# Loads issued only while about 1.4 MB of loads are under way, in a fused attention and two-layer kernel

## Chip, cores, metric

The kernel runs on one core of a Trainium2 chip. The metric is device time of one execution in microseconds (us); smaller is better. The profile is one profiled execution of the same program. Engines: PE does the matmuls, PEld is its weight load, DVE and ACT do vector work, POOL is GpSimd, and SP only issues DMAs and waits. A name with a q (SPq) is the sequencer of that engine.

## What is computed

Attention over chunks of 32 queries, each with 56 keys around it (16 to the left, 8 to the right) and 8 memory keys, for 4 batches, 8 heads, 768 positions, head width 64. Its output, 3072 tokens of 512, goes through two dense layers with a leaky activation. The reference, cut to what matters:

```python
for c in range(nc):                                   # 24 chunks of 32 queries
    q_c = q[:, :, c_start:c_end]
    k_full = np.concatenate([mem_k, k[:, :, l_start:r_end]], axis=2)
    v_full = np.concatenate([mem_v, v[:, :, l_start:r_end]], axis=2)
    scores = scale * np.matmul(q_c, k_full.transpose(0, 1, 3, 2))
    a = np.exp(scores - np.max(scores, axis=-1, keepdims=True))
    a = a / (np.sum(a, axis=-1, keepdims=True) + 1e-09)
    out[:, :, c_start:c_end] = np.matmul(a, v_full)
x = out.transpose(0, 2, 1, 3).reshape(B * S, H * D)   # 3072 x 512
h = x @ w_in                                          # 512 -> 2048
g = np.maximum(h, 0.0) + alpha * np.minimum(h, 0.0)
return g @ w_out                                      # 2048 -> 512
```

## The kernel before

**Attention.** The work is cut into 32 units: eight half sequences of 384 tokens times four pairs of heads. The first eight units (u < NWIN) take a path of their own, `windows`: score products on PE (`score_products`, L312, tile s_ps, with filler matmuls `stir`, L298, ahead of them), maximum, difference and sum on DVE, exponent on ACT (L517), scaling on POOL, a turn on PE (L546), two copies on ACT (L551), value products on PE (L559, tile a_ps), and a split of the result into a high part on ACT (xh, L474) and a low part on DVE (xl, L477). The other 24 units come later, spread over the dense layers (L337, L438).

**Dense layers.** The 2048 hidden columns are cut into 16 chunks f of 128. For a block of tokens and a chunk, PE makes h (12 matmuls, L723, 384 or 512 tokens wide) and adds to the output (L753). Every operand is two parts, high and low, so that three products stand for one. The first two blocks run jointly over the first nine chunks: (block 0, f), then (block 1, f - 1); then block 0 alone; then the others. Weights arrive as raw 64-bit words, 512 KB for a chunk of w_in and 512 KB for one of w_out, and are decoded once on ACT and DVE (`decode_part`, L622 to L649, first read of a load: L622) into parts that stay in the SBUF.

**Order.** Steps are entered into a `Plan` with a cost, what they read and write, and a due time. `Plan.send` lists them into one static order per engine before the program is built. At run time each engine goes through its list in that order and waits on semaphores; what stands behind a waiting instruction waits too.

**Loads.** All of them are issued by SP, in order:
- `load_first(u)` (L485): two loads for each of the first eight units from the tensor `first`: queries and keys (656 KB, here K0 to K7), and values (256 KB, here V0 to V7). They share four buffers `early`, so the loads of unit u + 4 wait until PE has read those of unit u. The DMA instruction is on L490.
- `load_w(f)` (L594): the two weight loads of chunk f (here I for w_in and O for w_out, each 512 KB), DMA on L599.
- alpha (8 KB), and for the later units `load_unit` (qvw and kw, L277, L280) and `load_v` (L290); the outputs at L818 and L822.

A DMA's completion is counted on one of eight semaphores in turn, and a DMA waits for the one that had its semaphore eight DMAs earlier.

SP's order at the beginning: K0, K1, K2, K3, K4, K5, V0, I0, K6, V2, V1, O0, K7, V4, V3, alpha, I1, V6, V5, I2, V7, O1, O2, I3, O3, I4, and on with weights.

Of the kernel before, what the change touches and what calls it, by code (L numbers as in the profile page):

```python
# [100 lines left out]


STIR = (8, 2, 1)

DUE_WEIGHTS, LAST_OUT = 4, 8

# [75 lines left out]
def body(ctx: ExitStack, tc: tile.TileContext, qvw, kw, first, w_in, w_out, alpha, out):  # L182
    nc = tc.nc
# [5 lines left out]
    at = ctx.enter_context(tc.tile_pool(name="at", bufs=1))  # L189
# [59 lines left out]
    def rest(place):  # L249
        wide = NNARROW * NF  # L250
        return (len(ORDER) - max(place, wide)) * WIDE_PAIR + max(wide - place, 0) * PAIR
# [5 lines left out]
    def due(u, later=0):  # L257

        return rest(begins(u) + later + (5.5 if u >= FIRST_FRONT else 0))
# [7 lines left out]

    def den_keys(u):
        return [("den", u % 3, n) for n in range(NJ * 2)]

    def load_unit(u):
        blk, pr = divmod(u, NPAIR)
        state[u] = {}
        i = sets(u)

        def load_q():
            nc.sync.dma_start(out=qs[i], in_=qvw[blk, pr, :, :BT])  # L277

        def load_k():
            nc.sync.dma_start(out=kbs[i], in_=kw[blk, pr])  # L280

        step(SP, 0.65, load_q, writes=[("q", i)], rest=due(u))
        step(SP, 0.81, load_k, writes=[("k", i)], rest=due(u))
# [11 lines left out]
    def stir(t, num):  # L295

        for _ in range(num):
            nc.tensor.matmul(out=t, lhsT=busy[:, :P], rhs=busy, start=True, stop=True)  # L298

    def score_products(u):  # L300
        blk, pr = divmod(u, NPAIR)
        st = state[u]
        s_ps = ps_s.tile([P, 512], F32, name="s_ps", tag=f"s{u % 2}")
        stir(s_ps, STIR[0] if u == 0 else STIR[1])
        st["s"] = s_ps[:, :2 * NJ * KW].rearrange("p (n k) -> p n k", k=KW)
# [45 lines left out]
    def scores(us):  # L351
        d = {}
        mk = ("mx", us[0] // len(us) % 2)

        def top(h2):
            if h2 == 0:
                d["mx"] = sm.tile([P, len(us), NJ, 2], F32, name="mx", tag=f"mx{len(us)}{mk[1]}")
            s = state[us[0]]["all"][h2]
            hide(us[0], s)
            nc.vector.tensor_reduce(out=d["mx"][:, :, :, h2], in_=s, axis=AX.X, op=ALU.max)  # L360

        def negate():
            nc.vector.tensor_scalar(out=d["mx"], in0=d["mx"], scalar1=-SCALE, scalar2=None, op0=ALU.mult)  # L363

        def exps(u, i):
            st = state[u]
            if i == 0:
                st["e"] = at.tile([P, NJ * 2, KW], F32, name="e", tag=f"e{u % 2}")
                st["den"] = sm.tile([P, NJ * 2, 1], F32, name="den", tag=f"den{u % 3}")
            n, h2 = divmod(i, 2)  # L370
            nc.scalar.activation(out=st["e"][:, i], in_=st["s"][h2][:, n], func=AF.Exp, scale=SCALE,  # L371
                                 bias=d["mx"][:, u - us[0], n, h2:h2 + 1], accum_out=st["den"][:, i])

        for h2 in range(2):
            step(DVE, 0.26 + 0.21 * len(us), partial(top, h2), writes=[("s", h2), mk], rest=due(us[0]))
        step(DVE, 0.17, negate, writes=[mk], rest=due(us[0]))
        for u in us:
            for i in range(NJ * 2):
                step(ACT, 0.54, partial(exps, u, i), reads=[("s", i % 2), mk],
                     writes=[("e", u % 2, i), ("den", u % 3, i)] if i else e_keys(u) + den_keys(u), rest=due(u))  # L380

    def weights(u):
        st = state[u]

        def guard():
            nc.vector.tensor_scalar(out=st["den"], in0=st["den"], scalar1=1e-9, scalar2=None, op0=ALU.add)

        def inverse():
            nc.vector.reciprocal(out=st["den"], in_=st["den"])  # L389

        def scale():
            nc.gpsimd.tensor_tensor(out=st["e"], in0=st["e"], in1=st["den"].broadcast_to([P, NJ * 2, KW]),  # L392
                                    op=ALU.mult)

        def spread():
            nc.scalar.copy(out=zeroed["e2"][:, :, NM:NM + CH], in_=st["e"][:, :, :CH])

        step(DVE, 0.16, guard, writes=den_keys(u), rest=due(u, DUE_WEIGHTS))
        step(DVE, 0.19, inverse, writes=den_keys(u), rest=due(u, DUE_WEIGHTS))
        step(POOL, 0.86, scale, reads=den_keys(u), writes=e_keys(u), rest=due(u, DUE_WEIGHTS))  # L400
        step(ACT, 0.37, spread, reads=e_keys(u), writes=["e2"], rest=due(u, DUE_WEIGHTS))
# [83 lines left out]
    def load_first(u):  # L485
        blk, pr = divmod(u, NPAIR)
        t = early[u % NSET]

        def load(lo, hi):
            nc.sync.dma_start(out=t[:, lo:hi], in_=first[blk, pr, :, lo:hi])  # L490

        state[u] = {}
        step(SP, 1.6, partial(load, 0, NQ + NT * NKT), writes=[("qk", u % NSET)], rest=due(u))
        step(SP, 0.78, partial(load, NQ + NT * NKT, NQ + NT * NKT + NV), writes=[("fv", u % NSET)], rest=due(u))

    def windows(u):
# [44 lines left out]
        def turn():  # L541
            st["t"] = [ps_o.tile([P, DM], F32, name="o_ps", tag=f"o{i}") for i in range(2)]
            stir(st["t"][0], STIR[2])
            for t in range(2):
# [43 lines left out]
    srcs = (w_in.bitcast(I32), w_out.bitcast(I32))  # L588

    raw = {}  # L590
# [3 lines left out]
    def load_w(f):  # L594
        def load(i):
            k, j = ((f, i), 0) if f < NAPART else ((f, 0), i)
            if k not in raw:
                raw[k] = wps[k].tile([P, 2 if f >= NAPART else 1, DM, 2], I32, name="w_t", tag="w")
            nc.sync.dma_start(out=raw[k][:, j].rearrange("p m b -> p (m b)"), in_=srcs[i][f])  # L599

        i = f - NF + NSET
        after = [("qk", i), ("fv", i)] if i >= 0 else []
        for i in range(2):
            step(SP, 1.31, partial(load, i), writes=[("r", f, i)] + after, rest=rest(place_of(f)))

    def place_of(f):
        return PLACE[0, f]
# [350 lines left out]
```

## Time and profile before

| what | us |
|---|---|
| three runs | 599.35, 599.86, 600.5 (median 599.86) |
| span of the profiled execution, from its first to its last instruction | 597.5 |
| median less span | 2.4 |
| PE busy in the span | 591.1 |

The profile has no other time of the profiled execution than its span; the 2.4 us are the median's distance from it, which holds what lies before the first and behind the last instruction. The granted clock of PE is 1.000. In the span 41.95 MB are read from HBM.

Start of the issue of the first loads, in us from the start of the span, by SP's rows:

| load | K0 | K1 | K2 | K3 | K4 | K5 | V0 | I0 | K6 | V2 | V1 | O0 | K7 | V4 | V3 |
|---|---|---|---|---|---|---|---|---|---|---|---|---|---|---|---|
| issued | 0.74 | 1.17 | 1.64 | 2.11 | 5.83 | 7.34 | 7.72 | 8.20 | 8.99 | 9.36 | 9.84 | 10.31 | 11.34 | 16.35 | 16.73 |

A row of the chain of work reads: start, length, what; it is followed back from the end to whatever released each step. A row of waits reads: who waited for whom, us in total, times, longest. A row of DMA issues gives the number of loads, the size of one and the median time from the start of its issue to its landing, when its semaphore is up.

### The profile page before, as it was taken

To read this page: it belongs to the slowest core of one execution; us is meant where nothing else is said; L and a number is where in the kernel's file an instruction comes from. 1 tells how busy PE (TensorE), PEld (TensorE's weight loads), DVE (VectorE), ACT (ScalarE), POOL (GpSimd) and SP (SyncE) were. 2 spreads that over 40 slices of the span, in tenths; PEclk is the share of its full clock that TensorE was granted. 3 is DMA by queue.
4 is the path that set the end of the run, shared out by engine and by line. 5 is a ranking of instruction groups with operands and counts; after the bars stand their busy time and mean duration, and the time that the engine had idled before them with its cause. 6 is when DMAs were issued, how large, how long until landed. Compare 5 with 4: busy or idle time off the path is not lost.

```text
span 597.5 us, 10975 instructions
## 1 busy us (share of the span) xinstructions
PE 591.1 (99%) x4430; PEld 505.7 (85%) x4430; DVE 386.7 (65%) x904; ACT 210.6 (35%) x580; POOL 36.5 (6%) x61
## 2 busy tenths in 40 slices
PE   8999999999999999999999999999999999999997
PEld 4789999888998989989898888888888888888885
DVE  5888898887959768685885852861862771530530
ACT  3788888644222504323233302302400411210201
POOL 3510000010001101010010100100100100000000
PEclk9999999999999999999999999999999999999999
DMA  8999500222040302403304003003101000000001
GB/s 337 359 399 407 226 0 1 66 65 89 2 152 2 101 23 79 153 1 100 94 8 150 4 1 100 2 0 109 62 2 36 1 0 36 36 1 0 1 1 71
DMA packets 21076, 48.96 MB, mean 82 GB/s; under 512 B 2464, under 2 KB 5792, under 8 KB 21024
## 3 DMA queue, kind: packets, MB, share of 16 engines
q1 hardware_dynamic: 20880, 48.12, 22.8%
q8 instruction: 35, 0.57, 0.4%
q14 instruction: 17, 0.14, 0.1%
q10 hardware_dynamic: 144, 0.13, 0.1%
HBM read 41.95 MB, written 6.29 MB: 81 GB/s over the span
## 4 chain that ended last, share of the span: by engine, by line
PE 96%; DMA 3%; SPq 0%; ACT 0%; issue 0%; ACTq 0%
PE h_ps L723 45%; PE o_ps L753 44%; PE a_ps L438 3%; DMA early<-first 3%; PE s_ps L337 2%; PE a_ps L559 1%; PE o_ps L546 1%; PE s_ps L312 0%; SPq L490 0%; PE o_ps L298 0%; ACT o_t L810 0%; PE s_ps L298 0%; ACTq L810 0%
## 5 line engine op out<-in xcount | busy, mean ns | idle before, releaser
L723 PE MATMUL h_ps<-xh,w 128*128 128x384 f32 (+1 forms) x896 | 248.8, 358 | 0.0
L723 PEld LDWEIGHTS h_ps<-xh,w 128*128 128x128 f32 x896 | 164.9, 188 | 16.0
L753 PE MATMUL o_ps<-w,gh 128*128 128x512 f32 x528 | 162.7, 389 | 0.0
L723 PE MATMUL h_ps<-xl,w 128*128 128x384 f32 (+1 forms) x448 | 162.6, 363 | 0.0
L732 ACT ACTIVATE g<-h_ps 128x384 f32<-128x384 f32 (+1 forms) x112 | 60.4, 540 | 194.7 <-PE h_ps L723 129.1
L735 DVE SCALAR_TENSOR_TENSOR g<-g,rise,h_ps 128x384 f32<-128x384 f32 (+1 forms) x112 | 74.7, 668 | 74.8 <-ACT g L732 74.1
L753 PEld LDWEIGHTS o_ps<-w,gh 128*128 128x128 f32 x528 | 99.1, 188 | 20.4
L413 DVE STREAM_TRANSPOSE pt<-e 32x64 f32<-32x64 f32 (+1 forms) x336 | 99.4, 301 | 7.4 <-POOL e L392 2.0
L753 PE MATMUL o_ps<-w,gl 128*128 128x512 f32 x264 | 102.8, 389 | 0.0
L723 PEld LDWEIGHTS h_ps<-xl,w 128*128 128x128 f32 x448 | 84.1, 188 | 10.2
L753 PE MATMUL o_ps<-w,xh 128*128 128x512 f32 x240 | 74.8, 393 | 0.0
L753 PEld LDWEIGHTS o_ps<-w,gl 128*128 128x128 f32 x264 | 49.6, 188 | 10.2
L477 DVE TENSOR_TENSOR xl<-a_ps,xh 128x384 fp32r<-128x384 f32 x32 | 17.6, 554 | 61.0 <-ACT xh L474 60.4
L753 PEld LDWEIGHTS o_ps<-w,xh 128*128 128x128 f32 x240 | 45.0, 188 | 8.9
L741 DVE CAST gh<-g 128x512 fp32r<-128x512 f32 (+1 forms) x72 | 28.8, 401 | 30.6 <-PE o_ps L753 28.2
L474 ACT CAST xh<-a_ps 128x384 fp32r<-128x384 f32 x32 | 15.0, 483 | 95.0 <-PE a_ps L438 93.7
L392 POOL TENSOR_TENSOR e<-e,den 128x384 f32<-128x384 f32 x24 | 22.8, 949 | 419.6 <-DVE den L389 270.0
L745 DVE TENSOR_TENSOR gl<-g,gh 128x512 fp32r<-128x512 f32 (+1 forms) x72 | 46.6, 648 | 1.7
L371 ACT ACTIVATE e<-s_ps,mx 128x64 f32<-128x64 f32 x144 | 43.4, 318 | 11.1 <-DVE mx L363 11.1
L753 PE MATMUL o_ps<-w,xl 128*128 128x512 f32 x120 | 46.8, 390 | 0.0
L371 ACT ACTIVATION_READ_ACCUMULATOR e<-s_ps,mx 128x1 f32 x144 | 30.4, 211 | 0.0
L810 ACT COPY o_t<-o_ps 128x512 f32<-128x512 f32 x21 | 12.2, 591 | 44.6 <-PE o_ps L753 44.2
(58 smaller groups left out, 380.2 us busy)
## 6 DMA issues: line engine op xcount, KB each, us to landing
w_t<-w_in SPq DMA_DIRECT2D x16, 512.0 KB, 10.0
w_t<-w_out SPq DMA_DIRECT2D x16, 512.0 KB, 10.1
qk<-kw SPq DMA_DIRECT2D x24, 272.0 KB, 4.3
v_t<-qvw SPq DMA_DIRECT2D x24, 256.0 KB, 2.8
out<-o_t SPq DMA_DIRECT2D x23, 256.0 KB, 2.1
early<-first SPq DMA_DIRECT2D x8, 656.0 KB, 6.2
qk<-qvw SPq DMA_DIRECT2D x24, 192.0 KB, 4.8
early<-first SPq DMA_DIRECT2D x8, 256.0 KB, 6.3
```

The costliest lines, as they stand in the source:

```text
L371: nc.scalar.activation(out=st["e"][:, i], in_=st["s"][h2][:, n], func=AF.Exp, scale=SCALE, bias=d["mx"][:, u - us[0], n, h2:h2 + 1], accum ...
L392: nc.gpsimd.tensor_tensor(out=st["e"], in0=st["e"], in1=st["den"].broadcast_to([P, NJ * 2, KW]), op=ALU.mult)
L413: nc.vector.transpose(out=pts[u % NPT][quad * CH:(quad + 1) * CH, j, t0:t0 + n1 - n0].rearrange("p t h q -> p (t h) q"), in_=(st["e"], zer ...
L438: nc.tensor.matmul(out=st["a"][h2 * D:(h2 + 1) * D, t * TQ:(t + 1) * TQ], lhsT=st["v"][:, t, h2, :], rhs=pts[u % NPT][:, :, t, h2, :], sta ...
L474: nc.scalar.copy(out=ring[k][0][:, cols], in_=st["a"][:, :BT])
L477: nc.vector.tensor_tensor(out=ring[k][1][:, cols], in0=st["a"][:, :BT], in1=ring[k][0][:, cols].bitcast(F32), op=ALU.subtract)
L723: nc.tensor.matmul(out=h["ps"][:, :n_cols], lhsT=ws[f, 0][:, wk, k * P:(k + 1) * P], rhs=parts(blk, k)[1](xk), start=(k == 0 and n == 0), ...
L732: nc.scalar.activation(out=h["g"], in_=h["ps"][:, :n_cols], func=AF.Relu, scale=-1.0)
L735: nc.vector.scalar_tensor_tensor(out=h["g"], in0=h["g"], scalar=rise[:, f:f + 1], in1=h["ps"][:, :n_cols], op0=ALU.mult, op1=ALU.add)
L741: copy(out=h["gh"], in_=h["g"])
L745: nc.vector.tensor_tensor(out=h["gl"], in0=h["g"], in1=h["gh"].bitcast(F32), op=ALU.subtract)
L753: nc.tensor.matmul(out=o_ps[tt], lhsT=h[gk][:, tt * P:(tt + 1) * P], rhs=ws[f, 1][:, wk], start=(f == first_f and i == 0), stop=(f == last ...
```

## The change

The loads of `load_first` and `load_w` go through a new function `bring`. It keeps a list of these loads with their sizes in KB, in the order of issue. For each new load it goes back through the list and adds up sizes; the load with which the sum reaches 1400 KB gets a dependency of the class Sync from the new one: the new load is issued only after that one has landed. Nothing else changes: not the steps, their costs, due times or order, nor the other loads.

```diff
+AHEAD = 1400
...
+    sent = []
+
+    def bring(out, in_, kb):
+
+        ins = nc.sync.dma_start(out=out, in_=in_).ins
+        ahead = 0
+        for name, size in reversed(sent):
+            ahead += size
+            if ahead >= AHEAD:
+                tc.add_manual_dep(ins, name, mybir.DependencyInfo(mybir.DependencyClass.Sync, mybir.DependencyReason.SCHED_ONLY),
+                                  reason="few loads at once")
+                break
+        sent.append((ins.name, kb))
...
-            nc.sync.dma_start(out=t[:, lo:hi], in_=first[blk, pr, :, lo:hi])
+            bring(t[:, lo:hi], first[blk, pr, :, lo:hi], (hi - lo) // 2)
...
-            nc.sync.dma_start(out=raw[k][:, j].rearrange("p m b -> p (m b)"), in_=srcs[i][f])
+            bring(raw[k][:, j].rearrange("p m b -> p (m b)"), srcs[i][f], 512)
```

With SP's order at the beginning this gives, by the sizes alone (the landing that a load waits for, and how many KB of the loads listed behind that one come before the new load):

| load | waits for | KB between | | load | waits for | KB between |
|---|---|---|---|---|---|---|
| K0, K1, K2 | none | | | V1 | I0 | 912 |
| K3 | K0 | 1312 | | O0 | I0 | 1168 |
| K4 | K1 | 1312 | | K7 | K6 | 1024 |
| K5 | K2 | 1312 | | V4 | V1 | 1168 |
| V0 | K3 | 1312 | | V3 | O0 | 912 |
| I0 | K4 | 912 | | I1 | O0 | 1168 |
| K6 | K5 | 768 | | V6, V5 | K7 | 1024, 1280 |
| V2 | V0 | 1168 | | weight after weights | third before it | 1024 |

## Prediction

> **What bounds the kernel now.** I read the page first, then the waits of PE, then the chain that ended last. From the page:
>
> ```profile
> span 597.5 us, 10975 instructions
> ...
> PE 591.1 (99%) x4430; PEld 505.7 (85%) x4430; DVE 386.7 (65%) x904; ACT 210.6 (35%) x580; POOL 36.5 (6%) x61
> ...
> DMA  8999500222040302403304003003101000000001
> ```
>
> PE is the bound. The loads, which are all that the change touches, fill the DMA engines only in the first four and a half slices of 14.9 us; after that the row shows mostly 0 to 4. So the question is what PE loses to loads in the first 65 us. The waits of PE, whole run:
>
> ```profile
> PE s_ps L298 <- DVE warm L224: 1.5, 1, 1.5
> PE a_ps L559 <- DMA early<-first: 0.4, 1, 0.4
> PE s_ps L298 <- DVE e L513: 0.4, 1, 0.4
> PE s_ps L312 <- DMA early<-first: 0.2, 1, 0.2
> ```
>
> PE is listed idle for a DMA only twice, 0.6 us together. That understates it, because filler matmuls (stir, L298) stand in front of the score products and hide waiting. The chain shows where landings set the pace (start, us, what):
>
> ```profile
> 1.64 6.35 DMA early<-first
> ...
> 9.84 9.18 DMA early<-first
> ...
> 19.06 0.88 PE a_ps L559 x16
> ...
> 35.27 0.89 PE h_ps L723 x4
> ```
>
> Up to 19.02 the chain hangs on two loads: K2, landed at 1.64 + 6.35 = 7.99, and V1, issued at 9.84 and landed at 19.02, for which the value products of unit 1 wait until 19.06. Behind that point every piece of the chain is PE work. So whatever the change does to landings before about 22 us can shift the end by as much; landings after it have room, as shown below.
>
> **What the queue does now.** The rows are stretches: busy us of PE, PEld, DVE, ACT, POOL, the clock, the DMA share, GB/s.
>
> ```profile
> 4.00:10.00 6.00, 5.61 (x91) 3.14 (x91) 3.73 (x11) 1.05 (x2) 0.74 (x2) 1.00 1.02 414
> 10.00:16.00 6.00, 5.64 (x102) 4.26 (x98) 3.96 (x14) 2.67 (x6) 2.71 (x9) 1.00 1.00 383
> 16.00:21.00 5.00, 4.58 (x68) 3.38 (x66) 4.60 (x11) 3.33 (x8) 1.82 (x4) 1.00 1.03 402
> 21.00:31.00 10.00, 10.00 (x125) 7.99 (x124) 8.46 (x20) 8.62 (x19) 5.61 (x14) 1.00 0.99 325
> 31.00:46.00 15.00, 15.00 (x104) 13.32 (x104) 13.19 (x22) 13.52 (x22) 0.74 (x1) 1.00 1.02 408
> ```
>
> The DMA engines are full all the time, at about 408 GB/s: 512 KB take 1.285 us, 656 KB 1.65, 256 KB 0.64. Next, issue to landing: the very first load K0; seven loads of w_in between 31 and 47 us; and the min, median and max of the 24 value loads of 256 KB of the later units, most of which go out into an empty queue:
>
> ```profile
> early<-first SPq DMA_DIRECT2D x1, 656.0 KB, 3.9
> ...
> w_t<-w_in SPq DMA_DIRECT2D x7, 512.0 KB, 10.2
> ...
> DMA to landing us min/median/max: 2.6/2.8/8.1
> ```
>
> A load alone needs its transfer and 2.0 to 2.25 us besides (2.6 - 0.64 and 3.9 - 1.65). A weight load takes 10.2 us because eight are under way: 10.2 / 1.285 = 7.9. All of these go out on SP's queue and land in the order of issue, so the 10.2 us are standing in line, not work.
>
> **The change part by part.** Nothing is removed or reordered: bring adds to each load a wait for an earlier landing. SP's queue keeps its order, so no load can overtake another and an urgent load cannot profit from a shorter line. A landing is then the later of two things: the landing before it plus its own transfer (as now), or its release plus 2.25 us plus its transfer. The second only counts if the loads still under way at the release last less than 2.25 us. By the rule of the diff, a release leaves 1312 KB under way (3.3 us) for K3, K4, K5 and V0; 912 KB (2.3 us) for I0, V1 and V3; 768 KB (1.93 us) for K6; 1168 KB (2.9 us) for V2, O0, V4 and I1; 1024 KB or more (2.57 us) for K7 and every weight load in a row of weight loads. The order, with K, V, I, O for queries with keys, values, w_in and w_out, is the one tabled above.
>
> So only K6 lacks cover, by 2.25 - 1.93 = 0.3 us; I0, V1 and V3 are even. Which of these could matter? Issues of K5, I0, K6, O0 and K7, and their times to landing in the same order; then PE's filler ahead of K6's and the products that read K7:
>
> ```profile
> 7.34 0.33 SPq L490 DMA_DIRECT2D early<-first  x1
> 8.20 0.44 SPq L599 DMA_DIRECT2D w_t<-w_in  x1
> 8.99 0.33 SPq L490 DMA_DIRECT2D early<-first  x1
> 10.31 0.65 SPq L599 DMA_DIRECT2D w_t<-w_out  x1
> 11.34 0.33 SPq L490 DMA_DIRECT2D early<-first  x1
> ...
> early<-first SPq DMA_DIRECT2D x1, 656.0 KB, 6.1
> w_t<-w_in SPq DMA_DIRECT2D x1, 512.0 KB, 7.8
> early<-first SPq DMA_DIRECT2D x1, 656.0 KB, 8.7
> w_t<-w_out SPq DMA_DIRECT2D x1, 512.0 KB, 10.0
> early<-first SPq DMA_DIRECT2D x1, 656.0 KB, 10.6
> ...
> 17.13 0.59 PE L298 MATMUL s_ps<-busy 128*128 128x512 bf16 x2
> ...
> 22.20 0.92 PE L312 MATMUL s_ps<-early 128*64 128x64 f32 x24
> ```
>
> They land at 13.4, 16.0, 17.7, 20.3 and 21.9. After the change:
> - **K6** is released by K5 at 13.4 and lands at 13.4 + 2.25 + 1.65 = 17.3, or after I0, 16.0 + 1.65 = 17.65. Both are at or before today's 17.7, since today's stream itself lost 16.0 - 13.4 - 0.64 - 1.285 = 0.7 us between K5 and I0. PE's filler ends at 17.72: room 0.0.
> - **V1**, on the chain, is released by I0 at 16.0: 16.0 + 2.3 + 0.64 = 18.9, or 0.64 each for V2 and V1 after K6, 17.7 + 1.28 = 19.0. Today 19.02.
> - **O0** and **K7**: 20.3, and 17.7 + 3.9 = 21.6 or 20.3 + 1.65 = 21.95. PE takes K7 at 22.20: room 0.25.
>
> Sum on the path: between -0.1 and +0.3 us; I take +0.1, for K6's and V1's covers are so near to the overhead that the slowest of 16 DMA engines may miss them.
>
> Off the path: ACT stands at the head of its queue for the first weights.
>
> ```profile
> ACT a L622 <- DMA w_t<-w_out: 1.6, 1, 1.6
> ...
> ACT a L622 <- DMA w_t<-w_in: 1.1, 1, 1.1
> ```
>
> Behind L622 wait xh (L474), exps (L517) and copies (L551); a later I0 or O0 would hold these back. Their landings, 16.0 and 20.3, come out unchanged, so this costs nothing; without that cover it is paid one to one, as the copies feed value products. SP itself gets up to 45 more semaphore waits, of 17 ns where one stands alone:
>
> ```profile
> L490 SPq EVENT_SEMAPHORE  x7: 17/17/28, 4.7 to 23.7; - x7
> ```
>
> That is below 1 us of a queue that mostly waits. Behind the waiting load stand al, the later units' kw and qvw, and output stores. When weights follow weights, a load waits for the third before it instead of the eighth: it goes out 5 x 1.285 = 6.4 us later and lands at the same moment, as 2.57 us of cover exceed 2.25. Were the cover too short, the nearest price is the stretch 21:31, 325 GB/s, and that is hidden:
>
> ```profile
> L337 PE MATMUL s_ps<-qk x1152: 212/216/241, 111.1 to 461.0; 64*32 64x64 f32 x192
> ...
> 58.93 2.08 PE o_ps L753 x9
> 61.01 2.10 PE h_ps L723 x12
> ```
>
> A block's chunk f takes 2.08 + 2.10 us, the two joint blocks 8.4 us per chunk, and its 1 MB lands in 2.57 us (3.2 at 325 GB/s); the later units are first read at 111.1, some 45 us after the last load of the dense part.
>
> On the overhead a page bears. The Trainium skill, "DMA: Bandwidth & Descriptors", section "Anatomy of one DMA", gives a DMA about 2.0 us fixed, mostly the receipt of the last write, plus bytes at 436 GB/s. The trace's 2.0 to 2.25 us agree. By the page's 2.0, K6 would lack 0.07 us instead of 0.3, and the sum would be 0.
>
> **Bounds of the unknown.** The trace has no gated load. At best the gate costs nothing and the lost 0.7 us come back: the chain then gains PE's 0.42 us at 19.06 and no more (0.4 in its row), as s_ps of unit 7 needs K7. At worst the early loads run as in 21:31, where SP had few loads under way because it waited for PE: from 10 us to 21.9 the queue moves 383 x 6 + 402 x 5.9 = 4670 KB, which at 325 GB/s take 14.4 us; K7 is 2.5 us late, PE 2.2 after its room. The measured pace with about 1.4 MB under way, K3 to K5, lies near the first end (414, then 383 GB/s), so I stay there.
>
> **The rivals.**
> 1. *Landings unmoved* (forecast), +0.1: 597.6 of its own profile, and the 2.4 us between span and median stay: **600.0**, by itself 599.2 to 600.8. Chance 0.60.
> 2. *The release comes too late* and DMA engines run dry between loads. It decides where issue to first useful byte exceeds the 1.93 to 2.57 us of cover. For it: 10:16 fell to 383 GB/s although 1.4 MB were under way, and 21:31 is the slowest stretch with the shortest queue. Against: full share of the DMA engines there too. +0.5 to +2.2: 600.4 to 602.1. Chance 0.24.
> 3. *The stream gets smoother*, -0.45: **599.4**. For it: 0.7 us lost in today's stream. Against: every landing after still has its own limit. Chance 0.09.
> 4. *The window drains before it is refilled*: 1312 KB would take 3.3 + 2.25 = 5.55 us, 242 GB/s; the 4670 KB then take 19.3 instead of 11.9 us: about 607. Against: each wait names one landing, three to five loads back. Chance 0.03. The Trainium skill, the same page, section "Bandwidth", wants 1 MiB or more per DMA for 75% of the peak, which would leave these 256 to 656 KB loads below it unless several overlap; the trace shows 408 GB/s with 512 KB loads, eight overlapped.
> 5. *The waits do nothing*, because no semaphore wait comes of the added dependency or because the eight-deep line already orders everything: 599.9. For it: nothing in the trace of before. Against: the dependency is of the class Sync, and 10.2 us to landing mean eight loads under way, far over 1.4 MB. Chance 0.04.
>
> **How the numbers follow.** About 0.2% (1.2 us) is what a measurement of this kernel can tell from no change. Slower by more: most of rival 2, rival 4, a little scatter: 0.25. Faster by more: no mechanism here reaches 1.2 us, so scatter and what I overlook: 0.06. Within: 0.69. The range goes from rival 3 less 0.5 us of the spread shown before (599.35 to 600.5) to rival 2's worst: 598.9 to 602.1.
>
> **What would show it.** Right: weight loads that take about 3.85 instead of 10.2 us to landing while 31:46 stays near 408 GB/s; V1 landing near 19.0; PE's wait at L559 near 0.4. Rival 2: 10:22 below 380 GB/s and longer PE waits at L312 or L559. Rival 3: V1 before 18.6. Rival 5: weight loads still at 10 us. I am wrong if PE's rows after 35 us change in length, for no load is on their path.

## The result: slower, and outside the forecast range

The changed kernel takes **604.19 us** in the median of 4 runs (601.94 to 605.71) against 599.81 us before (599.35 to 600.5): a ratio of 1.0071, 95% interval 1.0045 to 1.0097. The forecast was 600.0 with a range of 598.9 to 602.1; within 0.2% had the largest chance, slower 0.25.

The page of the changed kernel (its line numbers are 3 higher than before above `bring` and 17 higher below it, so that L298 is now L315, L312 is L329, L559 is L576, L723 is L740, L753 is L770, and all the early and weight loads are issued on L278):

```profile
span 603.9 us, 10978 instructions
...
PE 593.6 (98%) x4430; PEld 507.6 (84%) x4430; DVE 386.7 (64%) x904; ACT 210.7 (35%) x580; POOL 36.5 (6%) x61
...
DMA  8889940022122303223123102102300000100001
```

The span grew by 6.4 us. This profiled run is the longest of its four (605.71 us), so it shows the loss at its largest; the median grew by 4.4. DMA now falls short of 9 in the first slices and lasts nearly a slice longer. PE's waits:

```profile
PE s_ps L329 <- DMA early<-first: 3.9, 2, 2.6
PE s_ps L315 <- DVE warm L227: 1.5, 1, 1.5
PE s_ps L315 <- DVE e L530: 0.7, 2, 0.4
PE a_ps L576 <- DMA early<-first: 0.4, 1, 0.4
```

The 0.2 us for score products became 3.9 in two waits. The chain shows which loads they are:

```profile
8.22 5.64 DMA early<-first
...
13.93 5.94 DMA early<-first
...
19.93 7.11 DMA early<-first
...
27.09 1.22 PE s_ps L329 x24
...
41.73 2.80 PE h_ps L740 x15
```

These are K5, K6 and K7, landing at 13.9, 19.9 and 27.0; before the change they landed at 13.4, 17.7 and 21.9. K6 is now released by K5, and K7 by K6. K5 went out when PE had read the buffer that it takes, as before; it is late because it stands in line behind K3 and K4, and K3, which now waits for K0, landed at 10.6 instead of 9.6. The same 15 matmuls h_ps that began at 35.27 with a length of 2.80 now begin at 41.73, 6.46 later, and that is the whole difference of the spans. Behind that point nothing changed. The stretches that the prediction quoted:

```profile
4.00:10.00 6.00, 5.65 (x80) 3.40 (x79) 2.89 (x9) 0.63 (x2) 0.00 (x0) 1.00 0.98 369
10.00:16.00 6.00, 5.56 (x80) 3.69 (x81) 4.39 (x13) 3.09 (x7) 2.53 (x7) 1.00 0.89 335
16.00:21.00 5.00, 3.56 (x69) 2.72 (x65) 3.41 (x9) 2.65 (x6) 1.91 (x6) 1.00 0.94 307
21.00:31.00 10.00, 7.12 (x84) 5.50 (x86) 5.50 (x14) 5.23 (x10) 2.56 (x6) 0.83 0.81 265
31.00:46.00 15.00, 15.00 (x137) 12.65 (x134) 11.37 (x24) 11.59 (x23) 4.64 (x9) 1.00 0.88 293
```

Last three columns: granted clock, DMA share, GB/s. All five rates fell (414, 383, 402, 325, 408 before), and in 21:31 the clock of PE fell too, to 0.83. The DMA rows of K3, of K6, of K7 and of weight loads between 46 and 58 us:

```profile
early<-first SPq DMA_DIRECT2D x1, 656.0 KB, 5.9
...
early<-first SPq DMA_DIRECT2D x1, 656.0 KB, 5.9
...
early<-first SPq DMA_DIRECT2D x1, 656.0 KB, 7.1
...
w_t<-w_out SPq DMA_DIRECT2D x4, 512.0 KB, 4.8
w_t<-w_in SPq DMA_DIRECT2D x3, 512.0 KB, 5.0
```

Less 1.65 us of transfer, K3 needed 4.2 us besides, K6 4.3 and K7 5.5; weight loads, less 1.285, 3.5 to 3.7. The prediction had put 2.25 there, the price of a load that goes out alone.

### The profile page after: what moved, and what is told of

Same layout as the page of the kernel before. It is cut to its first block, busy times and chain, and to the rows that moved or that the text cites. A ratio compares the mean times of both kernels' runs of the same rounds, so it can differ in the third digit from the quotient of the medians.

```text
span 603.9 us, 10978 instructions
## 1 busy us (share of the span) xinstructions
PE 593.6 (98%) x4430; PEld 507.6 (84%) x4430; DVE 386.7 (64%) x904; ACT 210.7 (35%) x580; POOL 36.5 (6%) x61
## 4 chain that ended last, share of the span: by engine, by line
PE 96%; DMA 3%; ACT 0%; DVE 0%; issue 0%; SPq 0%; ACTq 0%
PE h_ps L740 44%; PE o_ps L770 44%; DMA early<-first 3%; PE a_ps L455 3%; PE s_ps L354 2%; PE a_ps L576 1%; PE s_ps L315 1%; PE s_ps L329 1%; PE o_ps L563 1%; PE o_ps L315 0%; ACT o_t L827 0%; DVE busy L208 0%; DVE warm L227 0%; SPq L278 0%; ACTq L827 0%
## 5 line engine op out<-in xcount | busy, mean ns | idle before, releaser
L740 PE MATMUL h_ps<-xh,w 128*128 128x384 f32 (+1 forms) x896 | 248.8, 358 | 0.0
L740 PEld LDWEIGHTS h_ps<-xh,w 128*128 128x128 f32 x896 | 164.9, 188 | 16.0
L770 PE MATMUL o_ps<-w,gh 128*128 128x512 f32 x528 | 162.8, 389 | 0.0
L740 PE MATMUL h_ps<-xl,w 128*128 128x384 f32 (+1 forms) x448 | 162.5, 363 | 0.0
L770 PEld LDWEIGHTS o_ps<-w,gh 128*128 128x128 f32 x528 | 99.1, 188 | 20.5
L770 PE MATMUL o_ps<-w,gl 128*128 128x512 f32 x264 | 102.8, 389 | 0.0
L740 PEld LDWEIGHTS h_ps<-xl,w 128*128 128x128 f32 x448 | 84.1, 188 | 10.2
L770 PE MATMUL o_ps<-w,xh 128*128 128x512 f32 x240 | 74.8, 393 | 0.0
L770 PEld LDWEIGHTS o_ps<-w,gl 128*128 128x128 f32 x264 | 49.6, 188 | 10.2
L494 DVE TENSOR_TENSOR xl<-a_ps,xh 128x384 fp32r<-128x384 f32 x32 | 17.7, 556 | 62.2 <-ACT xh L491 61.6
L770 PEld LDWEIGHTS o_ps<-w,xh 128*128 128x128 f32 x240 | 45.0, 188 | 8.9
L409 POOL TENSOR_TENSOR e<-e,den 128x384 f32<-128x384 f32 x24 | 22.7, 947 | 419.7 <-DVE den L406 270.1
L770 PE MATMUL o_ps<-w,xl 128*128 128x512 f32 x120 | 46.8, 390 | 0.0
```

What stands on the lines that cost most here:

```text
L494: nc.vector.tensor_tensor(out=ring[k][1][:, cols], in0=st["a"][:, :BT], in1=ring[k][0][:, cols].bitcast(F32), op=ALU.subtract)
L740: nc.tensor.matmul(out=h["ps"][:, :n_cols], lhsT=ws[f, 0][:, wk, k * P:(k + 1) * P], rhs=parts(blk, k)[1](xk), start=(k == 0 and n == 0), ...
L770: nc.tensor.matmul(out=o_ps[tt], lhsT=h[gk][:, tt * P:(tt + 1) * P], rhs=ws[f, 1][:, wk], start=(f == first_f and i == 0), stop=(f == last ...
```

## The experiments

Two theories stood at first. **A (cover)**: a load released while others move needs clearly more than 2.25 us besides its transfer, so the 0.8 to 1.3 MB left under way at a release run out before it arrives; a larger limit takes the loss away. **B**: each wait costs by itself, whatever is under way. Every kernel is the changed one with the edit shown; the ratio is to the kernel before, measured beside it.

### The limit: 2100, 2800, 1600, 700 and 400 KB

```diff
-AHEAD = 1400
+AHEAD = 2100
```

> AHEAD = 2100: five weight loads under way instead of three, the waits are as many. Theory A (cover): a load that is released while others move needs about 3.7 us besides its own transfer, so about 1 MB under way at the release (2.57 us) is too little and about 2 MB (5.1 us) is enough. Then weight loads land again every 1.3 us, K7 lands at 22 to 22.5 instead of 27.0, and the time is 599.8 to 600.6. Theory B (each wait costs by itself, whatever is under way): weight loads land every 1.7 us as with 1400, K7 stays at 25 us or later, and the time stays at 602 to 605.

599.61 us, ratio 0.9999 (0.9990 to 1.0009); K7 landed at 22.2.

> AHEAD = 2800: six weight loads under way. Theory A: no loss left, K7 lands at 22.0, time as before the change, 599.5 to 600.2. Theory B: 602 to 605, as with 1400.

600.04 us, ratio 1.0001 (0.9991 to 1.0010).

> AHEAD = 1600: four weight loads under way, 1536 KB (3.86 us) at a release, just above 3.7 us; K6 waits for K4 instead of K5. Theory A: weight loads again every 1.3 us, K7 at 22.7, time 599.8 to 600.8. If more than 3.7 us is needed, weight loads every 1.4 to 1.5 us and 601 to 603.

602.25 us, ratio 1.0043 (1.0026 to 1.0061): the second branch. 3.7 us was not enough as the price.

> AHEAD = 700: two loads under way. Theory A: cover of 1.3 to 1.65 us against some 3.7 us; K7 lands at 30 to 32, weight loads land every 2 to 2.5 us, time 608 to 612. Theory B: about the same number of waits as with 1400, 602 to 606.

610.52 us, one run.

> AHEAD = 400: a load waits for the one before it, so it goes out with nothing or 256 KB under way. Theory A1 (what is under way makes the 2.0 to 2.25 us of a lone load longer): weight loads take 3.3 to 3.6 us to landing, one at a time, about 150 GB/s. Theory A2 (a load that is released by a landing needs 3.7 us whatever is under way): 5.0 us each, 105 GB/s. Time 615 to 625 either way.

649.91 us, one run, far over both guesses of the time; but its weight loads issued into an empty queue are the point. The rows of its page, to landing:

```profile
w_t<-w_in SPq DMA_DIRECT2D x16, 512.0 KB, 3.5
w_t<-w_out SPq DMA_DIRECT2D x16, 512.0 KB, 3.5
```

Of these loads 26 went out with nothing else under way, and those alone have the same median. So a load released by a landing with nothing under way needs 3.5 - 1.285 = 2.2 us besides its transfer, about what lone loads did in the trace before (2.0 to 2.25). A1 holds: being released costs nothing, company does. The stretch 46 to 62 us, where weight loads follow weight loads, for 700, 1400 (the changed kernel), 1600 and 2100, one row from each kernel:

```profile
46.00:62.00 16.00, 15.25 (x79) 13.72 (x78) 11.98 (x20) 13.98 (x20) 0.00 (x0) 1.00 0.80 250
```

```profile
46.00:62.00 16.00, 16.00 (x81) 14.38 (x80) 14.76 (x22) 13.90 (x18) 0.00 (x0) 1.00 0.94 325
```

```profile
46.00:62.00 16.00, 16.00 (x82) 14.47 (x81) 14.40 (x22) 13.90 (x18) 0.00 (x0) 1.00 0.98 377
```

```profile
46.00:62.00 16.00, 16.00 (x82) 14.47 (x82) 14.40 (x20) 13.29 (x18) 0.00 (x0) 1.00 1.03 408
```

The last figure is the rate. With n loads of 524.3 kB under way, one of them just released, n x 524.3 / rate is the way of one load; less 1.285 us it is the price besides the transfer:

| limit KB | under way at a release | lasts us | GB/s | besides the transfer us | missing us |
|---|---|---|---|---|---|
| 400 | none | 0 | | 2.2 | 2.2 |
| 700 | 1 load | 1.3 | 250 | 2.9 | 1.6 |
| 1400 | 2 loads | 2.6 | 325 | 3.55 | 1.0 |
| 1600 | 3 loads | 3.9 | 377 | 4.3 | 0.4 |
| 2100 | 4 loads | 5.1 | 408 | hidden | 0 |

The price grows with what is under way, by about 0.55 us for each us of it, and the gap closes only at some 2 MB. Theory B is out: at 2100 the rule still makes 44 of the 48 loads wait, against 45 at 1400, and a weight load takes 6.4 us to landing instead of 10.2, so the waits act; but the loss is gone.

### Which loads

```diff
+    def bring(out, in_, kb, wait=True):
...
+            if wait and ahead >= AHEAD:
...
-            bring(raw[k][:, j].rearrange("p m b -> p (m b)"), srcs[i][f], 512)
+            bring(raw[k][:, j].rearrange("p m b -> p (m b)"), srcs[i][f], 512, wait=False)
```

> Only the loads of the first eight units wait; the weight loads go out without a wait of their own but count. Theory A with 3.7 us besides the transfer: K6 still waits for K5 and K7 for K6, so K6 lands at 18.9 to 19.9 and K7 at 24.3 to 26; time 601.5 to 604.5, most of the loss. Later weight loads run at 1.3 us each, off the path. Rival: the loss comes from the weight loads' waits, which hold SP's queue ahead of K6 and K7; then the time is below 600.5.

603.13 us, ratio 1.0052 (1.0036 to 1.0068). The reverse, wait=False for the loads of `first` alone:

> Only the weight loads wait (I0 for K4, O0 for I0, and all from I1 on); the eight units' loads go out as before but stand behind them on SP. Theory A: I0 lands at 16.9, O0, released by I0, at 21.9, K7 behind it at 23.5; time 600.5 to 602. Rival (a weight load's wait is the whole cost): 603 to 605.

601.06 us, ratio 1.0024 (1.0013 to 1.0036). And wait=f >= 2 for weights, False for the rest:

> Only the weight loads of chunks 2 to 15 wait; the eight units' loads and the weights of chunks 0 and 1 go out as before the change. Theory A: K6, V1 and K7 land as before the change (17.7, 19.0, 22.0); the later weight loads run at some 310 to 330 GB/s instead of 408 and that is hidden behind PE; time 599.3 to 600.2, no difference that can be told. Rival: slow weight loads do reach PE through ACT and DVE, which decode them; then 601 or more.

599.83 us, ratio 1.000 (0.999 to 1.001). Its stretch, beside the rows of 40 to 60 us of the kernel before and of this one:

```profile
40.00:60.00 20.00, 20.00 (x103) 18.25 (x102) 18.40 (x26) 17.07 (x23) 0.00 (x0) 1.00 1.03 407
```

```profile
40.00:60.00 20.00, 20.00 (x103) 18.23 (x102) 18.35 (x27) 17.08 (x23) 0.00 (x0) 1.00 0.94 323
```

K6, V1 and K7 landed at 18.4, 19.8 and 22.7 in the profiled run, 0.7 to 0.8 us after the expected moments although none of them waits for a landing; its span, 598.3, is 0.8 longer than that of before, so a single run scatters by about that much.

The waits of the eight units' loads cost 0.52%, those of the weight loads 0.24%; together 0.76%, against 0.71% for the change and 0.51% in its second set of runs below, so the split is rough, and that the two simply add is not shown. Of the weights only chunks 0 and 1 matter, for their waits hold SP's queue ahead of V1, K7 and what follows: with the weights' waits alone, K7 landed at 24.0. From chunk 2 on the same loss of rate (407 to 323 GB/s) does not reach PE, which is busy all 20 us in both.

### The clock of PE

```diff
-        stir(s_ps, STIR[0] if u == 0 else STIR[1])
+        stir(s_ps, STIR[0] if u == 0 else {6: 6, 7: 13}.get(u, STIR[1]))
```

> The changed kernel with 4 more filler matmuls ahead of the score products of unit 6 and 11 more ahead of those of unit 7, where PE stands idle 1.3 and 2.6 us for K6 and K7; the fillers end before these land. Theory C: part of the 6.4 us is no waiting but the clock that PE is granted after it stood idle (0.50 in 28 to 30 us), about 1.2 to 1.5 us; with PE kept busy the clock stays 1.00, and the span falls to 601.5 to 602.5 (time 603.3 to 604.3) in every run. If the clock is not worth that, span 603.5 to 604.

604.15 us, ratio 1.0071 (1.0056 to 1.0087); spans 601.8 to 602.8, the mean granted clock 0.999 to 1.000 in all four. The timeline of PE around unit 7, first of the changed kernel, then with the filler (start, length, then what; in brackets the idle time before):

```profile
27.09 1.22 PE L329 MATMUL s_ps<-early 128*64 128x64 f32 x24 [2.64 <-DMA early<-first]
...
28.64 1.49 PE L563 MATMUL o_ps<-eye,ew 128*128 128x128 f32 x6
30.05 1.29 PE L576 MATMUL a_ps<-qk,early 128*64 128x96 f32 x16
31.27 0.44 PE L740 MATMUL h_ps<-xl,w 128*128 128x384 f32 x1
```

```profile
26.81 0.92 PE L329 MATMUL s_ps<-early 128*64 128x64 f32 x24
...
27.88 0.82 PE L563 MATMUL o_ps<-eye,ew 128*128 128x128 f32 x6
28.63 0.88 PE L576 MATMUL a_ps<-qk,early 128*64 128x96 f32 x16
29.44 0.44 PE L740 MATMUL h_ps<-xl,w 128*128 128x384 f32 x1
```

From the score products of unit 7 to the first h_ps the changed kernel takes 4.18 us, with filler 2.63, which is what it took before the change (22.20 to 24.83). The rows of the clock in the changed kernel:

```profile
26.00:28.00 2.00, 0.91 (x24) 0.91 (x24) 0.06 (x1) 0.44 (x1) 0.91 (x3) 0.88 0.67 245
28.00:30.00 2.00, 2.00 (x13) 1.41 (x10) 1.09 (x3) 0.48 (x2) 0.00 (x0) 0.50 0.93 281
30.00:32.00 2.00, 2.00 (x21) 1.83 (x21) 1.22 (x4) 1.40 (x5) 0.25 (x1) 0.77 0.64 246
```

So 1.55 us of the 6.4 are no waiting but half the clock after it, and the remaining 4.9 are the delay of the products on K7 (22.20 to 27.09). The filler won nothing in the median because 13 of them last until 26.8, past K7's landing in that run, 25.6. The expectation had them end before it.

> The changed kernel once more, unaltered, for a second profile and more runs. Theory A: K6 lands at 19 to 20.5, K7 at 24.3 to 27; runs whose mean granted clock is 0.997 are 1.3 to 2.5 us longer than runs at 1.000, for PE stands idle long enough before K7 in these alone. Median 602 to 605.

603.01 us, ratio 1.0051 (1.0035 to 1.0068). K7 landed at 26.9 again. The part on the clock was only half right: in the two sets of the changed kernel the runs at 0.997 have spans of 603.5, 603.9 and 601.7, those at 0.999 to 1.000 have 600.0 to 602.1. PE's waits in this profile:

```profile
PE s_ps L329 <- DMA early<-first: 2.7, 3, 1.4
PE a_ps L576 <- DMA early<-first: 1.8, 1, 1.8
```

With waits up to 1.8 us this run kept a mean clock of 0.999; one of 2.27 us in the kernel with 1600 and the one of 2.64 us above were followed by 0.50. The length of a single wait does not decide it, though. With 700, PE stood idle for 1.59 us before 9.35 and for 1.22 us before 12.03, and the clock fell to 0.50 at 11.0; its row of 10 to 16 us:

```profile
10.00:16.00 6.00, 4.78 (x45) 3.18 (x41) 2.51 (x8) 1.04 (x3) 1.42 (x5) 0.59 0.79 252
```

With 400, two idle times of 1.64 and 1.56 us, 1.9 us apart, were not followed by 0.50 (before 45.28 and 48.74), so what decides stays open.

### By bytes or by number of loads

```diff
+            to = raw[k][:, j].rearrange("p m b -> p (m b)")
+            if f < 4:
+                bring(to, srcs[i][f], 512)
+                return
+            for x in (slice(0, DM), slice(DM, 2 * DM)):
+                bring(to[:, x], srcs[i][f][:, x], 256, 1280)
```

Here bring takes the limit as its last argument. The cut by rows takes slices of 64 rows instead.

> From chunk 4 on each weight load is cut into two loads of 256 KB (half the columns, 128 packets of 2048 bytes), with a limit of 1280 KB, so that a release leaves four small loads, 1024 KB, under way, the same bytes as two large ones. This is off PE's path; the rate in 48 to 60 us is what counts (313 GB/s in 40 to 60 with whole loads). If what lengthens a load's way goes by the bytes under way (3.72 us at 1024 KB), five small loads take 3.72 + 0.64 us: 301 GB/s. If it goes by the number of loads under way (2.0, 3.2, 3.7 and 4.3 us at none, one, two and three, so some 4.8 at four): 240 GB/s. Time within 1.5 us of the changed kernel.

602.83 us, one run.

> The same, cut by rows: 64 rows of 4096 bytes, 64 packets each, so that the packets under way are as many as with whole loads, 256. By bytes or by packets: about 300 GB/s. By the number of loads: about 240 GB/s. If this gives 300 and the cut by columns 240, it goes by packets.

602.42 us, one run. The stretch 48 to 60 us, cut by columns, then by rows:

```profile
48.00:60.00 12.00, 12.00 (x62) 10.86 (x61) 10.42 (x16) 10.14 (x13) 0.00 (x0) 1.00 0.88 292
```

```profile
48.00:60.00 12.00, 12.00 (x62) 10.86 (x61) 10.42 (x15) 10.13 (x12) 0.00 (x0) 1.00 1.04 235
```

292 GB/s by columns is near the 301 of the bytes and far from the 240 of the number of loads. The cut by rows is inconclusive: its 235 GB/s look like the answer "by number", but its DMA share is 1.04, so the engines did not run dry; loads of 64 rows simply move more slowly. By the records of single packets, 4096 bytes took 292 ns there in the median, and 159 ns in whole loads.

## Why the prediction was wrong

**The step that failed** is the term "its release plus 2.25 us plus its transfer". A landing is release, price and transfer, as it says, but the price was mis-sized and is no constant. The 2.25 us were measured on loads that go out alone and used for loads that go out behind 0.8 to 1.3 MB, where the price is 3.5 to 4.3 us, and 5.5 for K7. So "only K6 lacks cover", by 0.3 us, was wrong too: K6 came 1.1 us later behind the load before it than its own transfer takes, and K3, V0, K7 and the weight loads 0.9 us or more. With that, K6 is not at 17.3 to 17.65 but at 19.9, V1 at 21.2 instead of 18.9 to 19.0, and K7 at 27.0 instead of 21.6 to 21.95. The sum on the path, "+0.1", was 6.4 in the profiled run: 4.9 of delay, and 1.55 of slower clock, for which the sum had no term.

The trace before had the price. V7 goes out at 24.94 while V6, V5 and I2 are under way, 1 MB at most; first I2's row and V7's, then their issues:

```profile
w_t<-w_in SPq DMA_DIRECT2D x1, 512.0 KB, 4.7
...
early<-first SPq DMA_DIRECT2D x1, 256.0 KB, 4.8
```

```profile
22.88 0.43 SPq L599 DMA_DIRECT2D w_t<-w_in  x1
24.94 0.33 SPq L490 DMA_DIRECT2D early<-first  x1
```

I2 lands at 27.6, V7 at 29.7: 2.1 us behind it for 0.64 us of transfer, and 4.8 - 0.64 = 4.2 us besides the transfer. The nearest row to a gated load was this one, not a load into an empty queue.

**The evidence read the wrong way.** The prediction took 10:16, 383 GB/s, for the pace "with about 1.4 MB under way". By its own rows far more was under way: when O0 went out at 10.31, K5, V0, I0, K6, V2 and V1 had not landed, 2.6 MB. The load that did go out behind some 1.6 MB, K5 at 7.34, landed 2.2 us behind K4 for 1.65 us of transfer, which spoke for rival 2.

Against rival 2 the prediction held that 21:31 shows a full DMA share. It does, 0.99, but at 325 GB/s; 31:46 has 1.02 at 408. Share over rate is 3.05 against 2.50 per thousand GB/s: a byte kept an engine busy 22% longer. In a full share the loss is hidden inside packets. In the changed kernel 46:62 shows both parts: 0.94 / 325 is 2.89, 16% more per byte, and 0.94 instead of 1.02 is 8% idle. The trace's records of single packets show that the 16% lie in few of them. Of the packets of 4096 bytes there, 8.2% took over 250 ns, against 0.6% in 31:46 before, 2.9% with 1600 and 12.6% with 700 (46:62); the others took 160 to 162 ns on average in all four.

**Rival 2** named the right mechanism, with 0.24, and both of its signs came: 335 and 307 GB/s in 10:21, and 3.9 us of PE's waits at the score products. Its worst case, +2.2, was too small for two reasons: it took 325 GB/s as the floor, where 21:31 fell to 265, and it left out the clock, 1.55 us in the profiled run. So the range ended at 602.1, below the median.

**What held.** No load overtook another and nothing changed after 41.7 us. Slow weight loads later on are hidden: shown by waiting from chunk 2 on, 323 GB/s at a ratio of 1.000. That K6 and K7 have next to no room (0.0 and 0.25 us) was right, and is why the error came through: K7 landed 5.1 us later, and its products began 4.9 us later. Rival 4, a draining window, would have given 607; the changed kernel lies between. Rivals 3 and 5 fell: no landing came earlier, and the waits do act.

**What stays open.** Why company makes a load's way longer is shown only in part, for the profile lists no DMA engine by itself. That the first packets after an empty queue take longer stands in the packet records of the 400 kernel: in 24 of its 26 lone weight loads 34% of a load's first 32 packets took over 250 ns, and 2% of the other 96. That in the changed kernel some of the 16 engines run dry while others still have packets fits the share and the rate, but is argued, not tested. Nor is it shown why K7 took 7.1 and 7.2 us in the two profiles of the changed kernel and 5.3 to 5.6 in four other kernels in which it waits for K6 as well.

No kernel here beats the one before; limits of 2100 and 2800 and waits on the late weights alone equal it.

## What to carry to other kernels

Where loads land in the order of issue, as here, no load gets ahead by having fewer under way: no limit gained anything in these runs. A limit was free only where what is left at a release outlasts the way of a load in company, here about 2 MB, not the way of a lone load. Price a wait from a row in which the same thing happened under the same load, however rare that row is. And where a wait stands ahead of matmuls, add the clock that PE may lose after it.

## What the runs showed of the hardware

A load's price besides its transfer rose from 2.2 us alone to 4.3 us with 1.5 MB under way. Idle times of 2.27 and 2.64 us of PE were followed by a granted clock of 0.50 for 3.4 us; single ones up to 1.75 us were not, but two of 1.59 and 1.22 us, 1.5 us apart, were. Loads of 64 rows of 4096 bytes ran at 235 GB/s with all DMA engines busy, where 128 rows reach 408.
